# A gated S4 layer on one core: its hand-ordered list worked out anew, with the time steps' chain moved from VectorE to GpSimd

## The chip, the cores and the metric

The kernel runs on one core of one Trainium2 chip. The metric is the device time of one execution in microseconds; the figure given for a kernel is the median of its runs. The core's engines are named as in the profile: PE is the matrix engine (PEld its weight loads), DVE the vector engine, ACT the scalar engine, POOL the GpSimd engine, SP the engine that issues most DMAs. Each runs its own instructions in program order and waits for the others by semaphores.

## What is computed

A sequence of 2048 rows of 512 features is normalized row by row. One branch is a convolution along the sequence whose kernel is made from 512 x 128 complex parameters; the other is a feed-forward layer with 1792 hidden features. Their product is added to the input:

```python
xn = _layernorm(x, axis=-1)                       # x: (1, 2048, 512)
s  = _A_ref(xn, A_re, A_im, B_re, B_im, C_re, C_im, log_dt, Dskip)
#   dt = exp(log_dt); K[d,l] = Re sum_n C * dt*B * exp(dt*A*l); causal convolution of xn with K, + xn*Dskip
g  = _silu(_gelu(xn @ w1 + b1) @ w2 + b2)         # w1: 512 x 1792, w2: 1792 x 512
return x + s * g
```

## The kernel before

Three strands of work are woven into one list.

**Feed-forward.** x is cut into 4 tiles of 512 rows, the hidden features into 14 tiles of 128 (tiles 0 to 6 in a first pass over x, 7 to 13 in a second). Every float32 operand is split into a high and a low part, so that each product is three products of 128x128 with 512 columns ("wide products" below). Names in the code: `split` (L238, L240) casts a weight tile's high part on ACT and subtracts the low part on DVE, or on POOL where the list says so; `first_half` (L255 to L257) is 6 of the 12 products of a hidden tile, `first_start` (L265) the 12 of the very first; `gate` (L269) is gelu on ACT, `gate_high` (L275) the cast of its high part `hh`, `ffn_rest` (L281) the low part `hl` on DVE; `second_part` (L293 to L296) is 3 products into one of four sums `z`. Staging buffers for raw weights are four, so a load waits until an earlier tile has been split.

**Layer norm of x.** `ln_load` (L321) loads 128 x 2 rows, `ln_stat` (L326) takes statistics, `ln_root` and `ln_scale` normalize, `ln_store` (L356) stores the rows for the convolution, `ln_turn` (L368) transposes on PE, `ln_high` and `ln_low` (L377, L383) split. `ln_keep` (L387, L388) stores a whole split tile, 2 MB, from POOL's queue, for the second pass.

**The convolution's kernel.** `timestep` computes exp(log_dt) by a polynomial. `params` (token `P`) prepares the parameters of a block of 128 features on POOL, ACT and DVE, with six loads each. The generator then makes 32 sub-blocks: `gen_load` (`KL`), `gen_phase` (`A`, L599, PE), `gen_round` (`B`, L607 on ACT or L609 on DVE), `gen_wrap` (`C`, L613), `gen_size` (`Z`, L619 to L624, POOL), `gen_sin` (`N`, ACT), `gen_tables` (`E`, L645 to L652, DVE), `gen_sum` (`Q`, L660, PE), `gen_out` (`U`), `gen_keep` (`UD`).

The order of all this is the string `ORDER`: each token calls one of these functions, and the instructions of each engine follow each other as the tokens do. Nothing reorders them later. Before the list stands `prologue`, written out by hand: loads, dummy products on PE (`warm`), the time steps, the first x tile and the first hidden tile. The tokens met below: `F.j.h` first half h of step j; `G.j`, `H.j`, `R.j` gelu, high part, low part; `S.j.i` second half; `W.f`, `WB.f` the loads of w1 and w2 of hidden tile f; `WS.f.k` their four splits, a fourth number 1 meaning POOL; `LK.t` the store of a split x tile, `LL`, `LS`, `LD` load, statistics and store of rows; `B.s.h.o` rounds on DVE when o equals h and on ACT otherwise. After the list, from about 400 us on, the Fourier transforms of the convolution follow in a fixed order (`kernel_load` at L851 brings the finished kernel back, `side_skip` at L857 adds the skip, `first_dft` at L867 transforms).

Of the kernel before, what the change touches and what calls it, by code (L numbers as in the profile page):

```python
# [20 lines left out]
P = 128  # L21
# [30 lines left out]
WS.4.2 S.1.0 F.4.0 G.3 W.5 KL.0.0 H.2 H.3 LR.2 KL.0.1 S.1.1 KL.1.0 P.0 P.0 F.4.1 R.2 G.4 P.1 WS.3.3 LC.2  # L52
WS.4.3 S.1.2 S.1.3 S.2.0 Z.0 WB.5 S.2.1 TF.2.0 LC.3 A.0.0 TH.2.0 W.6 S.2.2 TF.3.0 R.3 LS.5.0 KL.1.1
B.0.0.1 H.4 WS.5.0 TL.2.0 C.0.0 S.2.3 S.3.0 WB.6 TH.3.0 WS.6.0 LS.4.0 TF.2.1 R.4 A.0.1 P.1 TL.3.0 S.3.1
S.3.2 B.0.1 WS.6.1 S.3.3 TH.2.1.1 WS.5.1 WS.5.2.1 TF.3.1 TL.2.1 S.4.0 C.0.1 WS.6.2 TH.3.1 TL.3.1 F.5.0
LS.5.1 N.0.0 A.1.0 F.5.1 B.1.0 F.6.0 C.1.0 A.1.1 N.0.1 LS.4.1 S.4.1 LR.4 B.1.1 LD.3 C.1.1 KL.2.0 G.5
E.0.0 E.0.1 N.1.0 E.0.2 F.6.1 S.4.2 G.6 LD.2 H.5 KL.3.0 R.5 S.4.3 H.6 A.2.0 F.7.0 B.2.0.1 F.7.1 LC.5
C.2.0 WS.5.3 F.8.0 N.1.1 Q.0 F.8.1 S.5.0 A.2.1 LC.4 S.5.1 G.7 WS.6.3.1 B.2.1 R.6 H.7 G.8 P.0 KL.2.1 Z.1
E.1.0 S.5.2 E.1.1 S.5.3 TF.4.0 C.2.1 S.6.0 E.1.2 TH.4.0 A.3.0 N.2.0 B.3.0.1 S.6.1 TL.4.0 F.9.0 Z.2 R.7
H.8 F.9.1 KL.4.0 U.0 O.0.0 C.3.0 KL.3.1 P.1 TF.4.1 S.6.2 A.3.1 G.9 P.1 F.10.0 O.0.2 B.3.1.1 O.0.1 C.3.1  # L60
LD.4 Q.1 N.2.1 S.6.3 A.4.0 R.8 F.10.1 O.0.3 E.2.0 S.7.0 Z.3 S.7.1 UD.0 E.2.1 E.2.2 LD.5 S.7.2 N.3.0 S.7.3
TH.4.1 H.9 S.8.0 U.1 UD.1 KL.5.0 B.4.0 LL.6 Q.2 N.3.1 S.8.1 G.10 R.9 C.4.0 TL.4.1 S.8.2 A.4.1 F.11.0
E.3.0 B.4.1 E.3.1 U.2 H.10 F.11.1 S.8.3 C.4.1 N.4.0 E.3.2 KL.4.1 R.10 P.1 TF.5.0 G.11 A.5.0 Q.3 TF.5.1
TH.5.0 S.9.0 S.9.1 B.5.0 KL.6.0 C.5.0 TL.5.0 LK.1 TH.5.1 F.12.0 TL.5.1 P.1 A.5.1 N.4.1 H.11 S.9.2 B.5.1
P.1 F.12.1 S.9.3 LL.7 C.5.1 F.13.0 P.1 KL.5.1 Z.4 G.12 N.5.0 H.12 R.11 P.1 S.10.0 P.1 S.10.1 LS.6.0
LS.6.1 N.5.1 F.13.1 S.10.2 G.13 F.14.0 KL.7.0 KL.6.1 P.1 LK.2 F.14.1 Z.5 R.12 S.10.3 A.6.0 U.3 F.15.0
S.11.0 E.4.0 E.4.1 G.14 E.4.2 B.6.0 C.6.0 LS.7.0 S.11.1 S.11.2 UD.3 UD.2 A.6.1 LS.7.1 Q.4 P.1 S.11.3
B.6.1 E.5.0 F.15.1 KL.7.1 Z.6 H.13 S.12.0 C.6.1 R.13 LR.6 E.5.1 A.7.0 H.14 F.16.0 E.5.2 S.12.1 B.7.0 OK.0
U.4 N.6.0 N.6.1 R.14 S.12.2 S.12.3 C.7.0 F.16.1 LC.6 P.2 E.6.0 G.15 P.2 E.6.1 S.13.0 P.1 S.13.1 Z.7 G.16
O.1.0 KL.8.0 A.7.1 F.17.0 LD.6 S.13.2 B.7.1 H.15 R.15 S.13.3 TF.6.0 F.17.1 H.16 C.7.1 O.1.1 KL.8.1 O.1.2  # L70
TH.6.0 G.17 A.8.0 TL.6.0 Q.5 P.2 O.1.3 E.6.2 TF.6.1 P.2 B.8.0 N.7.0 UD.4 R.16 U.5 TH.6.1 N.7.1 F.18.0
S.14.0 C.8.0 S.14.1 F.18.1 E.7.0 S.14.2 G.18 Q.6 A.8.1 S.14.3 S.15.0 LC.7 TL.6.1 B.8.1.1 Z.8 C.8.1 U.6
KL.9.0 W.7 P.2 S.15.1 WB.7 S.15.2 KL.9.1 H.17 TF.7.0 S.15.3 E.7.1 P.2 F.19.0 A.9.0 S.16.0 W.8 F.19.1 R.17
# [98 lines left out]
def kernel(  # L172
# [508 lines left out]
    def prologue():  # L681
# [17 lines left out]
        for n in range(2, 4):  # L699
            ln_load(n)  # L700
# [477 lines left out]
```

## Time and profile before

| | |
|---|---|
| time, median of 3 runs | 572.32 us (569.98 to 574.2) |
| the profiled execution | 573.57 us, of which the span from first to last instruction is 571.8 us |
| mean granted clock of PE | 0.99 |
| instructions | 17148 |

A page of the profile gives busy time by engine, the span in 40 slices, DMA queues, and groups of instructions by line. Views of the trace give the same for a stretch of time, the instructions in order, and for each idle stretch of an engine what ended it ("<-"). In the view by stretches the columns are the engines' busy times, the clock granted to PE (1.00 is full speed), the share of time that the DMA engines were busy, and GB/s. An engine with a small q behind its name is its sequencer, issuing a DMA.

### The profile page before, as it was taken

Reading aid. Unit: us, or ns where it says so; the run is one execution under the profiler, and the core shown is the slowest. Engines: PE = TensorE matmul, PEld = TensorE weight load, DVE = VectorE, ACT = ScalarE, POOL = GpSimd, SP = SyncE. Lnnn points to the kernel's source line nnn. Section 1 sums busy time; section 2 is a strip of 40 time slices with the busy share of each in tenths; the row PEclk is TensorE's granted clock in tenths of the full one; section 3 lists DMA queues with packets and bytes.
Section 4 is the critical chain, followed back from the end, with each engine's and each line's share of the span. In section 5 each row is a group of like instructions: output and inputs, shape, how many; then the busy total and the mean of one; then the engine's idle time right before and its main releaser. Section 6 shows DMA issues by size and latency. Waiting matters only on the chain. (4 is left out here: it accounts for less than half of the span.)

```text
span 571.8 us, 17148 instructions
## 1 busy us (share of the span) xinstructions
PE 545.7 (95%) x7187; PEld 436.7 (76%) x7187; DVE 468.6 (82%) x721; ACT 410.8 (72%) x599; POOL 282.5 (49%) x379
## 2 busy tenths in 40 slices
PE   8759999998999999999999999999999999999995
PEld 8548777766777777777777777777889988987883
DVE  6859999999998999999988988985357656766875
ACT  3538987987877999798998789698255556564542
POOL 0617483654874578969917746740320304114423
PEclk9889999999999999999999999999999999999999
DMA  8994235653376343474088106703976483625945
GB/s 189 263 294 133 74 92 206 211 192 89 114 279 223 130 139 97 162 204 74 4 270 293 47 21 147 147 10 101 381 288 77 129 134 77 188 51 120 206 114 110
DMA packets 99129, 86.92 MB, mean 152 GB/s; under 512 B 44294, under 2 KB 87562, under 8 KB 95980
## 3 DMA queue, kind: packets, MB, share of 16 engines
q1 hardware_dynamic: 94512, 65.37, 43.1%
q0 software_dynamic: 3424, 19.93, 10.1%
q8 instruction: 56, 0.92, 0.7%
q10 hardware_dynamic: 1116, 0.53, 0.4%
q14 instruction: 21, 0.17, 0.1%
HBM read 52.25 MB, written 33.55 MB: 150 GB/s over the span
## 5 line engine op out<-in xcount | busy, mean ns | idle before, releaser
L622 POOL TENSOR_TENSOR mm<-mm,rc 128x32 f32<-128x32 f32 (+4 forms) x150 | 112.9, 752 | 11.8
L255 PE MATMUL f<-xh,w1h 128*128 128x512 f32 x220 | 93.5, 425 | 5.8 <-ACT hf L269 5.8
L294 PE MATMUL z<-w2h,hh 128*128 128x512 f32 x224 | 97.8, 436 | 0.0
L257 PE MATMUL f<-xh,w1l 128*128 128x512 f32 x220 | 87.9, 399 | 2.5 <-DVE w1l L240 2.5
L295 PE MATMUL z<-w2l,hh 128*128 128x512 f32 x224 | 88.9, 397 | 0.0
L296 PE MATMUL z<-w2h,hl 128*128 128x512 f32 x224 | 88.5, 395 | 0.0
L256 PE MATMUL f<-xl,w1h 128*128 128x512 f32 x220 | 87.5, 398 | 0.0
L886 PE MATMUL s<-X,mc 64*64 64x128 f32 x2048 | 64.3, 272 | 1.1 <-issue 0.9
L903 DVE TENSOR_TENSOR t<-s,uh 128x512 f32<-128x512 f32 x64 | 41.1, 684 | 27.9 <-ACT uh L894 27.5
L886 PEld LDWEIGHTS s<-X,mc 64*64 64x64 f32 x2048 | 56.4, 133 | 5.4 <-issue 3.2
L281 DVE TENSOR_TENSOR hl<-hf,hh 128x512 fp32r<-128x512 f32 x56 | 50.5, 903 | 9.5 <-ACT hh L275 9.5
L619 POOL COPY mm<-rc 128x32 f32<-128x32 f32 x30 | 11.1, 370 | 91.5 <-DVE e L652 51.8
L255 PEld LDWEIGHTS f<-xh,w1h 128*128 128x128 f32 x220 | 42.0, 191 | 15.5 <-ACT hf L269 6.4
L257 PEld LDWEIGHTS f<-xh,w1l 128*128 128x128 f32 x220 | 41.8, 190 | 13.0 <-DVE w1l L240 2.9
L296 PEld LDWEIGHTS z<-w2h,hl 128*128 128x128 f32 x224 | 42.2, 189 | 10.4 <-DVE hl L281 0.4
L294 PEld LDWEIGHTS z<-w2h,hh 128*128 128x128 f32 x224 | 42.7, 191 | 9.3
L295 PEld LDWEIGHTS z<-w2l,hh 128*128 128x128 f32 x224 | 42.6, 190 | 8.2
L256 PEld LDWEIGHTS f<-xl,w1h 128*128 128x128 f32 x220 | 41.8, 190 | 8.9
L645 DVE TENSOR_TENSOR e<-mm,ra 128x1024 f32<-128x1024 f32 x32 | 44.4, 1388 | 4.2 <-ACT ra L633 3.9
L873 ACT COPY X<-s 128x512 f32<-128x512 f32 x56 | 28.9, 599 | 25.1 <-PE s L867 25.1
L613 DVE SCALAR_TENSOR_TENSOR ra<-ra,ph 128x512 f32<-128x512 f32 x64 | 43.6, 681 | 3.6 <-ACT ra L607 2.6
L269 ACT ACTIVATE hf<-f,b1s 128x512 f32<-128x512 f32 x56 | 38.5, 690 | 10.4 <-PE f L257 4.6
(181 smaller groups left out, 1161.9 us busy)
## 6 DMA issues: line engine op xcount, KB each, us to landing
x<-in_A_u_dram SPq DMA_DIRECT2D x16, 256.0 KB
xs<-x SPq DMA_DIRECT2D x16, 256.0 KB
xt_h<-xh POOLq DMA_DIRECT2D x4, 1024.0 KB, 6.1
xt_l<-xl POOLq DMA_DIRECT2D x4, 1024.0 KB, 8.1
kgd<-ko SPq DMA_DIRECT2D x32, 128.0 KB
za<-zo SPq DMA_DIRECT2D x4, 1024.0 KB
xh<-xt_h POOLq DMA_DIRECT2D x4, 1024.0 KB, 5.2
xl<-xt_l POOLq DMA_DIRECT2D x4, 1024.0 KB, 7.9
```

What stands on the lines that cost most here:

```text
L255: PE.matmul(p, wh[:, k, :], xh[:, k, :], start=(k == 0), stop=False)
L256: PE.matmul(p, wh[:, k, :], xl[:, k, :], start=False, stop=False)
L257: PE.matmul(p, wl[:, k, :], xh[:, k, :], start=False, stop=(k == KD - 1))
L281: V.tensor_sub(hl, hf, hh)
L294: PE.matmul(z, hh[:, s], wh, start=(f0 == 0 and not rows), stop=False)
L295: PE.matmul(z, hh[:, s], wl, start=False, stop=False)
L296: PE.matmul(z, hl[:, s], wh, start=False, stop=(f0 == FA - 1))
L613: V.scalar_tensor_tensor(ra[:, 0, c], ra[:, 1, c], MAGIC, p, op0=ALU.subtract, op1=ALU.subtract)
L622: GP.tensor_mul(mv[:, :, 0:3:2, w:2 * w], mv[:, :, 0:3:2, 0:w], rc[:, 2 + 2 * i:4 + 2 * i, :].rearrange("p j c -> p c j").unsqueeze(3).to_ ...
L645: V.tensor_mul(e1, m1.unsqueeze(1).to_broadcast([P, 2, CH, N1]), ra[:, :, :, :N1])
L886: PE.matmul(p[ka * 64:(ka + 1) * 64, r, o, :, jj], mc[h, k, ((0, 2), (1, 0))[c][o], :], xf[b][h, c, :, k, :], start=(c == 0), stop=(c == 1 ...
L903: V.tensor_mul(t, p[:, i, :, 1].unsqueeze(1).to_broadcast([P, 2, 2, P]), uh)
```

## The change

The list is written anew with the same tokens in another order, with a few marks changed. The hand-written part moves the time steps' arithmetic to POOL, runs 25 dummy products in place of 29, puts the load of the table `cbs` behind the parameters' and the next x rows, and takes the low row of b2 between the statistics.

```diff
 ORDER = """
-WS.0.3 LD.0 LD.1 WS.1.0 WS.1.1 P.0 P.0 W.2 G.0 H.0 WB.2 P.0 WS.1.2 W.3 BB P.0 R.0 P.0 WS.2.0 LS.3.0 F.1.0
-LL.4 LS.3.1 S.0.0 S.0.1 LS.2.0 WS.2.1 WS.1.3 WS.3.0 LS.2.1 WB.3 WS.2.2 S.0.2 F.1.1 LL.5 P.0 W.4 WS.2.3
-F.2.0 G.1 WS.3.1 H.1 WS.3.2 F.2.1 F.3.0 P.0 F.3.1 P.0 WB.4 S.0.3 P.1 WS.4.0 R.1 G.2 WS.4.1 P.0 LK.0 P.0
...
-S.52.2 S.52.3 G.55 R.54 S.53.0 UD.30 U.31 S.53.1 S.53.2 S.53.3 H.55 UD.31 R.55 KL0
+WS.0.3 LD.0 LD.1 P.0 WS.1.0 WS.1.1 P.0 P.0 WS.1.2.1 G.0 F.1.0 LS.2.0 W.2 LS.3.0 WB.2 H.0 W.3 P.0 WS.2.0
+LK.0 R.0 LL.4 LS.3.1 WS.1.3 P.0 WS.2.1 F.1.1 LS.2.1 G.1 WS.2.2 WS.2.3 P.0 S.0.0 WB.3 WS.3.0 W.4 WS.3.1
+S.0.1 H.1 F.2.0 S.0.2 F.2.1 G.2 WS.3.2 P.0 WB.4 H.2 W.5 WS.4.0 LL.5 F.3.0 P.0 WS.5.0 S.0.3 P.0 F.3.1 R.1
...
+N.31.1 E.31.0 U.29 E.31.1 G.54 F.55.1 Q.30 G.55 U.30 H.54 S.52.3 S.53.0 UD.29 E.31.2 Q.31 H.55 R.54 U.31
+S.53.1 S.53.2 S.53.3 UD.31 R.55 UD.30 KL0
 """
 def timestep():
...
-        V.tensor_scalar(x, p, -87.0, 88.5, op0=ALU.max, op1=ALU.min)
...
-        for c in (1.0 / 720, 1.0 / 120, 1.0 / 24, 1.0 / 6, 0.5, 1.0):
-            V.scalar_tensor_tensor(e, e, c, r, op0=ALU.add, op1=ALU.mult)
-            yield
...
+        A.copy(x, p)
+        yield
+        k, r, t, e = small("k"), small("r"), small("t"), small("e")
+        GP.tensor_scalar(x, x, -87.0, 88.5, op0=ALU.max, op1=ALU.min)
...
+        for c in (1.0 / 120, 1.0 / 24, 1.0 / 6, 0.5, 1.0, 1.0):
+            GP.tensor_mul(e, e, r)
+            GP.tensor_scalar(e, e, c, 1.0, op0=ALU.add, op1=ALU.mult)
...
 def prologue():
...
-        warm(29)
+        warm(25)
...
-        SY.dma_start(cbs, cb)
         next(pgen[0])
         for n in range(2, 4):
             ln_load(n)
+        SY.dma_start(cbs, cb)
         mv, rs = pair(0)
         bias_high()
-        for n in range(2):
-            ln_stats(n, mv[:, 2 * n:2 * n + 2, :])
+        ln_stats(0, mv[:, 0:2, :])
+        bias_low()
+        ln_stats(1, mv[:, 2:4, :])
...
-        bias_low()
         first_start(*steps[0])
```

In the whole list, 12 weight subtractions are marked for POOL, before 6; of the 64 roundings DVE has 38, before 41; the high parts of x on DVE are 3, before 2; two transposes of x take their bank from the generator's (`T`, before `TF`). The store LK.0 moves from behind F.3.1 to behind F.1.0 in the list, LK.1 from behind the fourth kernel sum (Q.3) to ahead of the first; the last weight load W.13 stands about 4 us of PE work before its cast, before about 12.6. b2's spread over the partitions (`BB`) and the second block's parameter loads move back.

More of the change, by code (lines that the diff above doesn't have):

```diff
@@ L54 @@
[L54 to L73, printed above, removed]
@@ new lines @@
+H.9 S.7.3 TH.4.1.1 KL.5.0 TF.5.0 KL.4.1 U.1 Q.2 TL.4.1 N.3.1 Z.3 A.4.0 TH.5.0 R.9 F.11.1 B.4.0.1 G.11
+E.3.0 LL.6 S.8.0 KL.5.1 TL.5.0 C.4.0 S.8.1 U.2 S.8.2 A.4.1 B.4.1 F.12.0 P.1 TF.5.1 TH.5.1 E.3.1 C.4.1
+S.8.3 E.3.2 S.9.0 A.5.0 P.1 N.4.0 UD.1 H.10 UD.2 B.5.0.1 C.5.0 H.11 KL.6.0 S.9.1 F.12.1 S.9.2 D Z.4 R.10
+A.5.1 S.9.3 G.12 P.1 H.12 TL.5.1 KL.6.1 LL.7 OK.0 S.10.0 Q.3 B.5.1 N.4.1 KL.7.0 S.10.1 P.1 R.11 S.10.2
+P.1 F.13.0 U.3 C.5.1 S.10.3 S.11.0 P.1 LK.2 LS.7.0 N.5.0 LS.6.0 N.5.1 E.4.0 S.11.1 P.1 E.4.1 S.11.2
@@ new lines @@
+A.8.1 UD.6 R.16 S.14.2 TF.6.1 KL.9.1 TL.6.0 F.18.0 OK.1 S.14.3 P.2 UD.5 P.2 B.8.1 C.8.1 N.7.1 F.18.1
+TH.6.1.1 S.15.0 A.9.0 TL.6.1 S.15.1 TF.7.0 E.7.0 H.17 S.15.2 E.7.1 E.7.2 P.2 G.18 B.9.0 C.9.0 S.15.3
+N.8.0 F.19.0 F.19.1 S.16.0 A.9.1 Z.8 TH.7.0.1 LD.7 N.8.1 Q.7 R.17 H.18 S.16.1 TL.7.0 S.16.2 KL.10.0
+B.9.1.1 C.9.1 G.19 LD.6 E.8.0 E.8.1 N.9.0 TF.7.1 S.16.3 U.7 F.20.0 H.19 W.7 A.10.0 KL.11.0 TH.7.1 KL.10.1
+S.17.0 F.20.1 E.8.2 Q.8 N.9.1 S.17.1 B.10.0 U.8 S.17.2 R.18 C.10.0 Z.9 S.17.3 G.20 TL.7.1 S.18.0 A.10.1
@@ new lines @@
+N.14.0 UD.10 E.13.1 W.11 UD.11 WS.8.2.1 U.12 E.13.2 S.25.1 N.14.1 KL.16.0 A.15.0 R.26 S.25.2 P.3 G.27
+F.28.1 KL.14.1 WS.9.1 XL.1 B.15.0 C.15.0 A.15.1 S.25.3 S.26.0 Z.14 F.29.0 WS.9.2 WS.10.1 S.26.1 WB.11
+S.26.2 B.15.1.1 KL.15.1 H.27 C.15.1 N.15.0 WS.8.3 G.28 H.28 UD.12 P.2 W.12 Z.15 F.29.1 Q.13 WS.11.0
+N.15.1 A.16.0 E.14.0 E.14.1 E.14.2 WB.12 F.30.0 R.27 KL.17.0 B.16.0.1 WS.11.1 S.26.3 WS.12.0 U.13 S.27.0
+C.16.0 KL.16.1 G.29 R.28 S.27.1 A.16.1 B.16.1 H.29 S.27.2 UD.13 WS.10.2.1 O.3.0 P.3 KL.18.0 F.30.1
@@ new lines @@
+E.19.1 A.21.0 S.34.2 H.36 ZA.0.2 R.36 G.37 F.38.0 F.38.1 N.20.0 S.34.3 Q.18 ZA.0.3 S.35.0 N.20.1 ZG.0
+KL.21.1 E.19.2 B.21.0 S.35.1 C.21.0 SL1.0 F.39.0 UD.16 S.35.2 E.20.0 S.35.3 U.18 G.38 XL.2 A.21.1 E.20.1
+E.20.2 Q.19 B.21.1 F.39.1 S.36.0 C.21.1 KL.22.0 U.19 S.36.1 A.22.0 H.37 R.37 H.38 N.21.0 Z.21 UD.19
+S.36.2 KL.23.0 R.38 G.39 B.22.0.1 C.22.0 Q.20 N.21.1 F.40.0 P.3 P.3 UD.18 A.22.1 S.36.3 F.40.1 H.39
+B.22.1 ZL.1 S.37.0 C.22.1 S.37.1 P.3 P.3 KL.22.1 P.3 F.41.0 U.20 G.40 E.21.0 F.41.1 S.37.2 KL.23.1 P.3
```

132 lines of the change are left out of this document (63 added, 69 removed).

## The prediction

> **What bounds the kernel now.** I read the busy shares first, then the same shares by stage with the granted clock, then the list of waits inside the worst stage, then the order in time around each wait.
>
> ```profile
> PE 545.7 (95%) x7187; PEld 436.7 (76%) x7187; DVE 468.6 (82%) x721; ACT 410.8 (72%) x599; POOL 282.5 (49%) x379
> ```
> ```profile
> 21.00:24.50 3.50, 2.88 (x7) 2.31 (x8) 3.43 (x7) 1.32 (x3) 2.89 (x7) 0.51 0.76 232
> 34.97:41.23 6.26, 0.51 (x3) 0.19 (x2) 0.61 (x1) 1.26 (x3) 0.22 (x1) 0.75 0.94 340
> 41.23:44.90 3.67, 3.67 (x9) 2.90 (x10) 3.39 (x13) 3.64 (x7) 2.83 (x7) 0.50 0.48 113
> 44.90:80.00 35.10, 35.10 (x224) 27.61 (x223) 34.47 (x60) 31.04 (x52) 22.36 (x29) 1.00 0.36 104
> 80.00:140.00 60.00, 54.93 (x538) 41.65 (x536) 57.19 (x92) 48.71 (x72) 34.04 (x53) 1.00 0.52 167
> 140.00:400.00 260.00, 259.64 (x2652) 199.22 (x2650) 234.13 (x308) 224.75 (x289) 167.44 (x214) 1.00 0.47 137
> 400.00:571.80 171.80, 161.85 (x3619) 139.77 (x3617) 110.61 (x166) 86.34 (x156) 44.22 (x50) 1.00 0.62 156
> ```
> Columns: stretch and length, then busy time of PE, weight load, DVE, ACT and POOL, granted clock, DMA share, GB/s. From 140 to 400 us PE has no gap (259.64 of 260): that stage costs what its products cost, and the new list has the same products. After 400 us the code is the same. So the list can win or lose in the first 140 us, or by starving PE where it is full now. Between 80 and 140 us PE is idle for 5.07 us while DVE is at 95%. The rest of the loss is in the first 45 us:
>
> ```profile
> ACT w1h L238 <- DMA w1s<-in_B_w_dram: 10.6, 3, 6.3
> PE f L255 <- ACT hf L269: 5.8, 1, 5.8
> PE f L257 <- DVE w1l L240: 2.5, 1, 2.5
> 27.09 0.54 SPq L221 DMA_DIRECT2D w1s<-in_B_w_dram  x1
> 28.00 0.76 POOL L387 DMA_DIRECT2D xt_h<-xh  x1
> DMA to landing us min/median/max: 11.5/11.5/11.5
> 39.97 0.62 ACT L238 CAST w1h<-w1s 128x512 fp32r<-128x512 f32 x1 [6.26 <-DMA w1s<-in_B_w_dram]
> ```
> PE's 5.8 us end with ACT's gelu (L269), but the gelu stood behind the cast of weight tile 4, which waited for its load: issued at 27.09, usable at 39.97, 12.9 us. One microsecond after it POOL issued the store of the first x tile (LK.0, L387 and L388); the landing row is the store of its low part, issued at 28.76, so it ended at 40.2. The load came in with the store, not before. The clock column adds a second cost: 0.51 after the wait at 21.6, 0.50 after the one at 41.2.
>
> ```profile
> 26.49 0.39 PE L255 MATMUL f<-xh,w1h 128*128 128x512 f32 x1
> 33.48 0.40 PE L294 MATMUL z<-w2h,hh 128*128 128x512 f32 x1
> 41.82 0.63 PE L256 MATMUL f<-xl,w1h 128*128 128x512 f32 x1
> 44.38 0.63 PE L295 MATMUL z<-w2l,hh 128*128 128x512 f32 x1
> 45.10 0.39 PE L255 MATMUL f<-xh,w1h 128*128 128x512 f32 x1
> ```
> The first two rows are 30 wide products apart: 0.233 us each. The next two are 6 apart: 0.427 us each at half clock. Before 45.10, 74 wide products have been issued. My sum compares the time of that 74th.
>
> **The change part by part.** *Start.*
>
> ```profile
> 4.56 8.07 PE L430 MATMUL warm<-ident 128*128 128x128 f32 x58
> 4.67 0.16 DVE L466 TENSOR_SCALAR sm_x<-sm_turn 128x4 f32<-128x4 f32 x1 [3.03 <-PE sm_turn L464]
> 7.01 0.69 DVE L326 BATCH_NORM_STATS2 bst<-x 128x6 f32<-128x512 f32 x1
> 12.80 2.03 PE L368 MATMUL xT<-ident,x 128*128 128x128 f32 x16 [0.17 <-DVE x L351]
> 15.60 1.20 PE L265 MATMUL f<-xh,w1h 128*128 128x512 f32 x4 [0.78 <-ACT xh L377]
> 0.00:5.00 5.00, 3.49 (x15) 3.25 (x16) 1.04 (x7) 1.67 (x3) 0.84 (x7) 1.00 0.56 136
> ```
> DVE's chain of 13 small operations for the time steps runs from 4.67 to 7.09, and the statistics of x start right behind it without waiting for data. By 5 us the DMAs have moved 136 GB/s x 5 = 680 KB, so the first x tile (512 KB, first in SP's queue) is in; the second follows by about 7. Without the chain, DVE has 2.3 us more, of which the row correction of b2 (0.68, moved between the statistics) takes part, and the second x tile the rest. The 25 warm products (50 of the 58 passes, 8.07 x 50/58 = 6.96) end at 11.5 instead of 12.6. I put the transposes at 11.55, 1.25 earlier (bounds 0.5 and 1.3, the warm products' end), and the first tile's product at 14.35.
>
> The chain itself is now 22 POOL operations. No such shape ran there:
>
> ```profile
> L857 POOL TENSOR_TENSOR in<-in,dsk x8: 227/228/232, 406.6 to 490.9; 128x16 f32<-128x16 f32 x8
> L530 POOL TENSOR_SCALAR pr_h<-pr_h 128x128 f32<-128x128 f32 x8 | 4.3, 533 | 0.7
> 14.19 0.46 POOL L500 TENSOR_TENSOR pr_wr<-pr_cr,pr_br 128x128 f32<-128x128 f32 x1 [12.74 <-DMA pr_br<-in_A_B_re_dram]
> 28.09 0.35 DVE L535 SCALAR_TENSOR_TENSOR pr_ci<-pr_ci,sm_dt,pr_br 128x128 f32<-128x128 f32 x1 [1.27 <-POOL pr_br L532]
> ```
> Between 22 x 0.228 = 5.0 and 22 x 0.533 = 11.7 us from 4.9 on; I take 0.25 each (nearest in size), so it ends near 10.5, inside POOL's wait until 14.19 (about 13.3 now that the table cbs is loaded behind the parameters). The result is first used at 28.09. At nothing, then; at the upper bound it delays POOL by 3 us. Its extra ACT copy lies in ACT's wait for b2.
>
> *First tile.*
> ```profile
> 20.87 0.69 DVE L240 TENSOR_TENSOR w1l<-w1s,w1h 128x512 fp32r<-128x512 f32 x1
> L240 POOL TENSOR_TENSOR w1l<-w1s,w1h x1: 1279/1279/1279, 52.2 to 52.2; 128x512 fp32r<-128x512 f32 x1
> 18.97 0.93 SPq L221 DMA_DIRECT2D w1s<-in_B_w_dram  x1
> 23.88 0.62 ACT L238 CAST w1h<-w1s 128x512 fp32r<-128x512 f32 x1 [2.17 <-DMA w1s<-in_B_w_dram]
> ```
> Weight tile 1's low part (L240, waited for 2.5 us by PE) goes from DVE at 20.87 to POOL, behind six parameter operations (6 x 0.533 = 3.2 us from 13.3): 16.5 + 1.3 = 17.8, just as PE asks for it. That wait goes. PE then runs both tiles' 24 products and three of the second half, 27 x 0.233 = 6.3, to 20.65. Next late is hl of tile 0, which now stands on DVE behind two statistics of x: about 21.5 by an estimate (DVE's six parameter operations from 16.9 on, 2.3 us, two statistics of 0.69 with their 0.18, and hl's 0.7), a wait of 0.85. Four more products end at 22.4. Then PE wants weight tile 2, which before came at 23.88 and now has LK.0 in its way: the store is moved up past tile 2's and 3's loads, to POOL's turn at about 18.0, a moment before SP issues the load at 18.97 (SP's pace there is set by the four stores of xs, which don't move).
>
> What that costs is not shown; bounds: at best it lands as now (23.9); at worst with the end of LK.0, as weight tile 4 did: 18.75 + 11.5 = 30.2. I take 27.5, since the store's bytes are few beside the load's in the first microseconds: in the old place its 2 MB took until 40.2 with all queues full. Cast and start: 28.2, a new wait of 5.8 us for PE. It brings the half clock with it: about 8 products at 0.427, 1.6 us more. The other 43 products to the 74th take 10.0. The loads of tiles 3 and 4 (tile 4 now ahead of b2b and of x 5, which is 0.75 MB less) come in behind the same store while PE works, and I let them cost nothing beyond; uncovered, each microsecond counts fully. 74th: 28.2 + 1.6 + 10.0 = 39.8, against 45.1: **5.3 us gained**; 2.6 with tile 2 at 30.2; 9 with it at 23.9, where tile 4 holds it.
>
> The Trainium skill, page "DMA: Bandwidth & Descriptors", section "Queues, rings and completion order", says that each DMA engine takes turns between the queue rows packet by packet. By that the load on SP's row would share with POOL's store and land well before its end, and the sum would be near the 9; the 12.9 us of weight tile 4 speak against it.
>
> *The rest of the list.* DVE gives up the chain, 6 of 21 weight subtractions (POOL then has 12) and 3 of 41 roundings (to ACT), and takes one cast of x from ACT:
>
> ```profile
> L609 DVE TENSOR_SCALAR ra<-ph 128x512 f32<-128x512 f32 x41 | 28.1, 686 | 8.2 <-PE ph L599 6.6
> L240 DVE TENSOR_TENSOR w1l<-w1s,w1h 128x512 fp32r<-128x512 f32 x9 | 7.0, 774 | 5.7 <-ACT w1h L238 5.7
> L240 POOL TENSOR_TENSOR w2l<-w2s,w2h 128x512 fp32r<-128x512 f32 x3 | 4.8, 1593 | 1.2 <-ACT w2h L238 1.2
> ```
> 6 x 0.77 + 2 x 0.69 = 6.0 us less on DVE beside the chain, some 3 of it due before 140 us. DVE set PE's 5.07 us of idle there, so I book 1.5 of those (from -3, if POOL's 6 x 1.6 = 9.6 us delay the size tables or LK.1, the second x tile's store, moved up from behind the fourth kernel sum to ahead of the first, delays the generator's loads, to +4).
>
> The Trainium skill, page "SBUF — State Buffer", section "Who interferes with whom", says a POOL operation that reads SBUF and a DVE operation with two SBUF inputs block each other for a whole instruction. By that the six moved subtractions would hold DVE for up to 6 x 1.3 = 7.8 us and undo their 4.6, which leads to the given-back rival below. The trace agrees as far as POOL's 1.593 us in the mean against 1.279 for the single one; it does not show who blocked whom.
>
> *End of the list.*
> ```profile
> 397.24 1.10 PE L660 MATMUL kg<-e,e 128*32 128x64 f32 x64
> 407.92 0.23 POOL L857 TENSOR_TENSOR in<-in,dsk 128x16 f32<-128x16 f32 x1 [1.13 <-DMA in<-kgd]
> 411.14 2.01 PE L867 MATMUL s<-fc,in 32*128 32x64 f32 x64
> ```
> After the last kernel sum (397.24) there were seven second-half blocks, now three: the first transform that needs the reloaded kernel comes 4 x 0.7 = 2.8 us sooner after that sum. Its input was ready 3.0 us ahead (408.15 against 411.14). The slack is used up; I book 0.5 (0 to 3).
>
> Sum: 5.3 + 1.5 - 0.5 = 6.3 us. The profiled execution took 573.57 us (span 571.8, 1.8 around it), so 567.3 on its scale; it lies 1.25 above the median of 572.32, so **566.0**.
>
> **The rivals.**
> *The load shares with the store* (tile 2 at 23.9): 9 + 1.5 - 0.5 = 10 us, 562. For it: tile 2's load, issued at 18.97, took 4.9 us in a full queue. Against: tile 4's 12.9.
> *The loads land with the store's end*: gain 2.6 + 0 - 0.5, 570. For it, the same 12.9; against, that the store starts among bytes of xs still to be moved.
> *The front's gain is given back*: DVE, 98% busy from 44.9 to 80 and 95% to 140, does not follow, and PE waits there for what it gained: 572. Against: DVE itself idled at 34.97 to 41.23 (0.61 busy).
> *Slower: a second-half load is caught.* The last weight tile (W.13) is now cast about 4 us of PE work after its issue, before 12.6 (counted in the list, 0.7 us a block). If a 1 MB transfer is under way, it takes 12.9 as tile 4 did: ACT stands 9 us with gelus behind it, PE waits as at 34.97, plus half clock (9 x 0.19 = 1.7): 573.57 - 6.3 + 10.7 = 578, 577 on the median's scale. It decides once that load takes more than some 10 us. Against: tile 12 had 3.9 us of cover before, and ACT waited for no weight load after 45 us (13.5 us in all, 10.6 of them between 15 and 45 and 2.9 at 8.99).
>
> **How the numbers follow.** Chances: forecast 0.45, sharing 0.17, store's end 0.14, given back 0.10, slower 0.14. A measurement here can tell about 1% (5.7 us) from no change. The forecast's own range is 562 to 570; the range 558 to 576 takes in the bounds 562 less the +4 of the middle, and most of the slower case. Faster by over 1%: two thirds of 0.45, and 0.17: 0.48. Slower by over 1%: 0.14 and a remainder of the given-back case, 0.16. Within 1%: 0.36.
>
> **What would show it.** Right: transposes at 11.5 to 12; no wait of PE on L240's low part of tile 1; a wait of some 3 to 8 us for tile 2 at 22, with a clock near 0.5 behind it; none of 5 us at tile 4; the 74th wide product near 40; PE full from 140. Wrong: a wait on a weight cast after 45 us, PE idle over 8 us between 80 and 140, or DVE under 90% there with PE waiting.

## The result and the profile after

The changed kernel takes 578.63 us (median of 4 runs, 578.27 to 583.11), the kernel before 572.08 in the same comparison: a ratio of 1.014, with a 95% interval of 1.010 to 1.018. The prediction was 566.0 in a range of 558 to 576. The change costs 6.5 us where 6.3 were to be gained.

The profiled execution took 583.11 us (span 581.3), the longest of the four; the others lie 4 to 5 us below it. The view by stretches, with the columns as before (busy time of PE, PEld, DVE, ACT, POOL; granted clock, DMA share, GB/s), shows where it went:

```profile
24.50:35.60 11.10, 4.25 (x10) 3.34 (x11) 3.41 (x11) 3.85 (x6) 2.02 (x6) 0.54 0.91 255
45.00:80.00 35.00, 34.05 (x259) 25.79 (x261) 34.17 (x57) 30.53 (x51) 22.75 (x34) 1.00 0.64 192
80.00:140.00 60.00, 59.46 (x590) 45.91 (x578) 56.41 (x97) 51.22 (x78) 44.16 (x59) 1.00 0.37 118
140.00:250.00 110.00, 109.94 (x1014) 84.80 (x1018) 104.39 (x131) 97.08 (x133) 85.52 (x103) 1.00 0.54 177
250.00:262.00 12.00, 9.97 (x155) 7.87 (x152) 11.10 (x15) 7.27 (x9) 8.46 (x10) 0.86 0.54 86
281.00:305.00 24.00, 15.76 (x178) 11.77 (x178) 12.37 (x25) 12.90 (x17) 7.50 (x12) 0.79 0.70 209
305.00:400.00 95.00, 95.00 (x881) 72.99 (x880) 78.61 (x102) 82.32 (x100) 53.79 (x72) 1.00 0.40 104
```

Three of these stretches have a clock under 1.00: the front, 250 to 262, and 281 to 305. In the last PE is busy for 15.76 of 24 us, and a mean clock of 0.79 means that (1 - 0.79) x 24 / 0.5 = 10 us of it ran at half speed. Before, PE was busy for all 24 there. Between 80 and 140, on the other hand, PE is now busy for 59.46 of 60 us (54.93 before).

How far each kernel is at a given piece of work shows gains and losses better than busy shares do. The table gives the start of the n-th wide product in us, from the two traces in order of time. The lists put other work between the products in another order, so differences of 1 to 2 us inside the list mean little; the 1344th stands eight before the list's last in both (the count takes in the eight products that add b2).

| wide product | 1 | 24 | 40 | 74 | 100 | 400 | 800 | 850 | 950 | 1344 | span |
|---|---|---|---|---|---|---|---|---|---|---|---|
| before | 15.6 | 25.1 | 28.8 | 44.8 | 52.0 | 142.6 | 255.1 | 268.9 | 295.6 | 413.1 | 571.8 |
| after | 15.5 | 20.9 | 34.9 | 44.4 | 53.0 | 140.1 | 249.5 | 268.2 | 306.6 | 422.5 | 581.3 |
| after - before | -0.1 | -4.2 | +6.1 | -0.4 | +1.0 | -2.5 | -5.6 | -0.7 | +11.0 | +9.4 | +9.5 |

The front gains 4.2, loses 10.3 and wins 6.5 back; the middle gains 6.6; and between products 800 and 950 the kernel loses 16.6 us, all of it after 250 us, where the kernel before had no gap. From the 1344th product on the two are alike (158.8 and 158.7 us).

The list of waits, PE's three largest (in all, how often, the longest), and SP's longest in the window from 262 to 300 us:

```profile
PE ph L596 <- DMA lh<-pcd: 8.2, 1, 8.2
PE f L256 <- ACT w1h L239: 7.6, 1, 7.6
PE ph L596 <- DMA rc<-recd: 2.0, 1, 2.0
```
```profile
SPq L447 <- ACT ko L663: 17.1, 1, 17.1
```

The first is `lh`, the 24 KB that `gen_load` brings for sub-block 22. It is small, and PE waits 8.2 us for it. The timeline of SP, which issues it, tells why (start, duration of the issue; after first, then before):

```profile
265.87 0.33 SPq L667 DMA_DIRECT2D kgd<-ko  x1
283.13 5.41 SPq L447 DMA_DIRECT2D gd<-zi  x4
288.64 2.30 SPq L588 DMA_DIRECT2D rc<-recd  x1
290.98 1.46 SPq L819 DMA_DIRECT2D raw<-xs  x1
292.49 2.81 SPq L667 DMA_DIRECT2D kgd<-ko  x1
295.40 0.68 SPq L582 DMA_DIRECT2D lh<-pcd  x1
```
```profile
268.20 0.68 SPq L585 DMA_DIRECT2D lh<-pcd  x1
...
286.39 4.79 SPq L446 DMA_DIRECT2D gd<-zi  x4
291.27 1.90 SPq L585 DMA_DIRECT2D lh<-pcd  x1
```

L447 is `z_store`, the second half of token `ZG.0`: four stores of 256 KB of what a silu on ACT has just made. SP comes to them at 266.2, stands 17 us until the silu is done, and issues nothing meanwhile. (The list of waits names ACT's copy to `ko`; the silu, L441 below, ended at 283.11, and the first store went out at 283.13.) Behind them in the new list stand `KL.21.1` (`rc`, the seeds of a size table), `SL1.0` (`raw`), `UD.16` (`kgd<-ko`, the store of a finished kernel block) and `KL.22.0` (`lh`). In the old list `KL.22.0` stood ahead of `ZG.0` and went out at 268.20. On ACT and PE the same thing is seen from the other side:

```profile
281.19 1.92 ACT L441 ACTIVATE zi<-zi 128x2048 f32<-128x2048 f32 x1
285.46 0.69 ACT L604 ACTIVATE ra<-ph,mag 128x512 f32<-128x512 f32 x1
297.08 0.37 ACT L663 COPY ko<-kg 128x256 f32<-128x256 f32 x1 [10.93 <-DMA kgd<-ko]
297.68 0.61 PE L596 MATMUL ph<-cbs,lh 96*128 96x512 bf16 x1 [8.24 <-DMA lh<-pcd]
```

ACT too stands 10.9 us, at `U.18`: its output buffer `ko` (two of them) is free only when `UD.16`'s store is through. And one more load is in play: `XL.2`, the reload of an x tile (2 MB on POOL's queue), starts at 282.3, ahead of these loads, where in the kernel before `lh` had gone out 17 us ahead of it (268.20 and 285.10). So two theories stood at this point. *SP's order*: one store that waits for an engine holds every load behind it in SP's queue. *The bytes*: 2 MB of reload and 1 MB of stores under way at once are what delays them. The front's loss (LK.0, as the prediction feared) was the second thing to test.

### The profile page after: what moved, and what is told of

Same layout as the page of the kernel before. It is cut to its first block, busy times and chain, and to the rows that moved or that the text cites. A ratio compares the mean times of both kernels' runs of the same rounds, so it can differ in the third digit from the quotient of the medians.

```text
span 581.3 us, 17142 instructions
## 1 busy us (share of the span) xinstructions
PE 545.8 (94%) x7179; PEld 435.7 (75%) x7179; DVE 461.2 (79%) x700; ACT 411.6 (71%) x601; POOL 296.9 (51%) x407
## 3 DMA queue, kind: packets, MB, share of 16 engines
q1 hardware_dynamic: 94512, 65.37, 42.7%
q0 software_dynamic: 3424, 19.93, 10.2%
## 4 chain that ended last, share of the span: by engine, by line
PE 57%; DVE 20%; ACT 6%; DMA 5%; issue 5%; SPq 4%; POOL 1%; DVEq 0%; POOLq 0%; ACTq 0%
PE s L883 7%; PE z L295 7%; PE z L296 6%; PE z L297 6%; PE f L256 5%; PE f L257 5%; PE f L258 5%; PE kg L657 4%; PE s L864 4%; PE sa L918 3%; DMA w2s<-in_B_w_dram 2%; DVE hl L282 2%; PE ph L596 2%; PE w L936 2%; DVE ra L610 1%
## 5 line engine op out<-in xcount | busy, mean ns | idle before, releaser
L619 POOL TENSOR_TENSOR mm<-mm,rc 128x32 f32<-128x32 f32 (+4 forms) x150 | 114.3, 762 | 11.8
L295 PE MATMUL z<-w2h,hh 128*128 128x512 f32 x224 | 99.0, 442 | 0.0
L282 DVE TENSOR_TENSOR hl<-hf,hh 128x512 fp32r<-128x512 f32 x56 | 49.1, 882 | 13.1 <-ACT hh L276 13.0
L616 POOL COPY mm<-rc 128x32 f32<-128x32 f32 x30 | 10.9, 364 | 80.5 <-DVE e L649 53.7
L295 PEld LDWEIGHTS z<-w2h,hh 128*128 128x128 f32 x224 | 42.9, 191 | 11.1 <-issue 2.3
L297 PEld LDWEIGHTS z<-w2h,hl 128*128 128x128 f32 x224 | 42.5, 190 | 11.5 <-DVE hl L282 1.0
L296 PEld LDWEIGHTS z<-w2l,hh 128*128 128x128 f32 x224 | 42.7, 191 | 8.2
L642 DVE TENSOR_TENSOR e<-mm,ra 128x1024 f32<-128x1024 f32 x32 | 46.1, 1439 | 1.0 <-ACT ra L630 0.5
```

Source lines behind the costliest of these rows:

```text
L282: V.tensor_sub(hl, hf, hh)
L295: PE.matmul(z, hh[:, s], wh, start=(f0 == 0 and not rows), stop=False)
L296: PE.matmul(z, hh[:, s], wl, start=False, stop=False)
L297: PE.matmul(z, hl[:, s], wh, start=False, stop=(f0 == FA - 1))
L619: GP.tensor_mul(mv[:, :, 0:3:2, w:2 * w], mv[:, :, 0:3:2, 0:w], rc[:, 2 + 2 * i:4 + 2 * i, :].rearrange("p j c -> p c j").unsqueeze(3).to_ ...
L642: V.tensor_mul(e1, m1.unsqueeze(1).to_broadcast([P, 2, CH, N1]), ra[:, :, :, :N1])
```

## The experiments

All kernels are compared with the kernel before on the same chip; its median was 571.0 to 572.2 us in the three groups of runs.

**Three tokens ahead of the silu's stores (a_keys).**
```diff
-... N.20.1 ZG.0 KL.21.1 E.19.2 ... F.39.0 UD.16 ... C.21.1 KL.22.0 U.19 ...
+... N.20.1 KL.21.1 UD.16 KL.22.0 ZG.0 E.19.2 ... F.39.0 ... C.21.1 U.19 ...
```


> The changed kernel with three tokens moved: KL.21.1 (load of the size table's seeds), UD.16 (store of a finished kernel block) and KL.22.0 (the load lh of sub-block 22) stand ahead of ZG.0 instead of behind it. Theory, SP's order: in the changed kernel SP stands from 266.2 to 283.1 at the four stores of ZG.0, which wait for the silu, and then issues seed load, raw load, block store and lh one behind the other until 295.4; PE, which wants lh at 289, stands 8.4 us and then runs 10 us at half clock. With the three ahead of the silu both go: product 950 comes no later than product 850 against the kernel before (now it loses 11.7 us between them), and the time is 578.6 - 11.7 = 567. Rival, the bytes: the reload of an x tile (XL.2, 2 MB) and the silu's 1 MB under way from 282 on are what holds the loads; then the wait moves to the next load or to ko's store and at least half of the loss stays: 573 or more.

Measured: 569.27 us (10 runs), ratio 0.997 (0.994 to 1.000). Product 850 stands at -1.4 against the kernel before, product 950 at +0.1. Between the two the kernel loses 1.5 us where the changed kernel loses 11.7, and SP's timeline has the three ahead of the stores:
```profile
265.64 0.38 SPq L588 DMA_DIRECT2D rc<-recd  x1
266.08 0.45 SPq L667 DMA_DIRECT2D kgd<-ko  x1
271.23 0.66 SPq L582 DMA_DIRECT2D lh<-pcd  x1
282.48 5.28 SPq L447 DMA_DIRECT2D gd<-zi  x4
```
SP still stands 11 us before the silu, and PE waits for nothing there. (The profiled execution of this kernel, 579.6 us, is the longest of its ten. Of its excess 6.6 us lie behind the list, with 10.2 us at half clock from 427 on, which the median does not show.)

**The reload later (a_xl).**
```diff
-... U.18 G.38 XL.2 A.21.1 ... S.36.1 A.22.0 H.37 ...
+... U.18 G.38 A.21.1 ... S.36.1 A.22.0 XL.2 H.37 ...
```


> The changed kernel with one token moved: the reload XL.2 (2 MB on POOL's queue) stands behind A.22.0 and no longer ahead of it, as in the kernel before; SP's order is that of the changed kernel. Theory, SP's order: SP still issues nothing between 266 and 283 and lh stands behind ZG.0's stores; only the issues after 288.6 (2.30, 1.46 and 2.81 us where such an issue takes 0.3 to 0.6 elsewhere) become quicker, by at most 5 us. PE still stands 3 to 5 us at sub-block 22, and the time is 574 to 577. Rival, the bytes: without the reload the loads come in time, PE doesn't stand there, and the time is 567.

Measured: 580.73 us, ratio 1.014 (1.009 to 1.018), the changed kernel's. PE waits as long as ever:
```profile
PE ph L596 <- DMA lh<-pcd: 8.5, 1, 8.5
```
The expectation, 574 to 577, missed as well: POOL has nothing to do between the two places, so the reload's two issues went out at 281.08 and 281.69, no later against the rest than in the changed kernel (282.34 and 282.95), and the slow issues behind the stores stayed. This run shows that the token's place doesn't matter, not what the kernel would do without those bytes. The bytes as the cause by themselves fall by the run above: there the reload is where the changed kernel has it, and the loss is gone. A share in it they may have: behind the stores the three issues ahead of `lh` took 6.6 us together in the changed kernel, where such an issue mostly takes 0.3 to 0.6, so by an estimate some 5 of the 8.2 us are slow issues. They matter only for what stands behind the stores, and no run takes the bytes away.

**The reverse, in the kernel before (b_zg).**
```diff
-... A.21.1 KL.22.0 ZA.0.3 ... P.3 ZG.0 H.38 A.22.0 ...
+... A.21.1 ZA.0.3 ... P.3 ZG.0 KL.22.0 H.38 A.22.0 ...
```


> The kernel before with one token moved: KL.22.0 (lh of sub-block 22) stands behind ZG.0, whose four stores wait for the silu, and no longer ahead of it. Nothing else of the change is in it. Theory, SP's order: lh is issued at about 291.2, behind the stores (they end there in the kernel before), and lands 2.2 us later; A.22.0 wants it at 285.7, so PE stands 7 to 9 us and then runs 3.4 to 10 us at half clock, 2 to 5 us more: 571.6 + 10 to 13 = 582 to 585. Rival, that the late wait of the changed kernel needs its other moves too (the reload XL.2, UD.16's store): then PE stands less than 3 us and the time is 575 or less.

Measured: 583.65 us, ratio 1.021 (1.015 to 1.026): one token makes the kernel before 11.5 us slower, without anything else of the change. The token now stands two ahead of its use, so this run alone does not tell the stores from the short distance; a_actq below does.
```profile
PE ph L599 <- DMA lh<-pcd: 10.9, 2, 10.6
```
Product 900 stands at -3.4 and product 950 at +9.3: 12.7 us lost at this place.

**The load of sub-block 22 alone (a_kl22).**
```diff
-... N.20.1 ZG.0 KL.21.1 ... C.21.1 KL.22.0 U.19 ...
+... N.20.1 KL.22.0 ZG.0 KL.21.1 ... C.21.1 U.19 ...
```


> The changed kernel with KL.22.0 alone ahead of ZG.0; the block store UD.16 and the seed load KL.21.1 stay behind it. Theory: PE's wait of 8.4 us for lh goes, but ACT still stands at ko (U.18) until UD.16's store has landed near 297, with the casts of hh behind it, and POOL at the seeds until 295.7; PE runs out of second halves some 5 us later and stands 3 to 6 us for hl. About half of the 11.7 us comes back: 572 to 574, and PE's wait there is on DVE's hl or ACT's hh. Rival, lh alone made the loss: no wait over 2 us between 280 and 305, and the time is that of the kernel with all three moved, 569.

Measured: 579.17 us, ratio 1.012 (1.007 to 1.016). Nothing came back that the measurement could tell, where I had expected half; neither forecast time was met. The wait moved:
```profile
ACT ko L663 <- DMA kgd<-ko: 10.9, 1, 10.9
DVE hl L282 <- ACT hh L276: 10.4, 1, 10.4
PE kg L657 <- ACT ko L663: 7.1, 1, 7.1
```
The next kernel sum (`kg`, one PSUM buffer) needs ACT's copy of the sum before it, the copy needs a `ko` buffer, and that buffer's store is `UD.16`, still behind the silu. The mechanism was right, its way to PE was another (the sum's buffer, not `hl`), and its size was 7.1 us rather than 3 to 6. Both things behind `ZG.0` cost PE about the same 7 to 8 us; to move one of them gains nothing.

**The stores on ACT's queue (a_actq).**
```diff
-            (GP if t == NTB - 1 else SY).dma_start(gd[b]...
+            (GP if t == NTB - 1 else A).dma_start(gd[b]...
```


> The changed kernel with its own list; the four stores of a ZG go out on ACT's queue, behind the silu that makes them, and not on SP's. Theory, SP's order: SP no longer stands at the silu, so seeds, raw rows, ko's store and lh go out as they come due, and PE's wait of 8.4 us at sub-block 22 goes without any token moved; ACT pays some 1 to 5 us for issuing the four, of which PE sees little. The time is 568 to 572. Rival, the bytes or the list's order itself: the wait stays above 4 us and the time is 575 or more.

Measured: 574.83 us, ratio 1.006 (1.002 to 1.009); against the changed kernel's 1.014, so by the medians rather more than half comes back with the list untouched, though the time is 3 us above the 572 expected at most. PE no longer waits for `lh`, whose token still stands three ahead of its use: SP issues it 20 us before PE comes to it (290.72). But ACT pays for issuing the stores, seen in its timeline and in PE's waits:
```profile
270.12 0.68 SPq L582 DMA_DIRECT2D lh<-pcd  x1
281.38 4.93 ACTq L447 DMA_DIRECT2D gd<-zi  x4
```
```profile
PE kg L657 <- ACT ko L663: 3.1, 1, 3.1
```
Four issues hold ACT 4.9 us, the upper end of the price that I had set (1 to 5 us); "of which PE sees little" was wrong, PE waits 3.1.

**The store of x at its old place (a_lk).**
```diff
-... WS.2.0 LK.0 R.0 LL.4 ... F.3.1 R.1 P.0 WS.4.1 ...
+... WS.2.0 R.0 LL.4 ... F.3.1 R.1 P.0 LK.0 WS.4.1 ...
```


> The changed kernel with one token moved: LK.0 (the 2 MB store of the first split x tile) stands behind R.1, as in the kernel before, and no longer ahead of the loads of weight tiles 2 and 3. Theory: weight tile 2 lands near 24 as in the kernel before and not at 30.6; PE's wait of 7.6 us and two of its three stretches at half clock go, product 74 comes at 35 to 38 (now 44.4), and most of it stays to the end: 569 to 573. Rival, given back: DVE, busy 34.17 of 35 us between 45 and 80, does not follow; product 74 comes early but product 400 at 139 or later, and the time is 577.

Measured: 575.99 us, ratio 1.007 (1.005 to 1.010), 2.6 us below the changed kernel. Product 74 comes at 36.2 as expected, PE's wait for tile 2 is 0.8 us; but product 100 comes at 47.8: of 8.2 us gained, 5.2 are left. Product 400, at 134.4, still has them, as the first theory said; the time, expected at 569 to 573, lies nearer to the rival's 577. Part of the difference is that the changed kernel's profiled execution is 4.5 us above its median, so that a gain read against it is too large.

**The store of x moved up, in the kernel before (b_lk).**
```diff
-... BB P.0 R.0 P.0 WS.2.0 ... WS.4.1 P.0 LK.0 P.0 ...
+... BB P.0 LK.0 R.0 P.0 WS.2.0 ... WS.4.1 P.0 P.0 ...
```


> The kernel before with one token moved: LK.0 stands ahead of R.0, POOL's sixth parameter operation behind it, so that POOL issues the 2 MB store at about 17.5, as in the changed kernel. Theory, the loads land with the store's end: weight tile 2 comes at 30 to 31 in place of 23.9, PE stands 6 to 8 us there and none at weight tile 4 (now 5.8); one wait for another, product 74 at 44 to 47 (now 44.8), the time 571 to 574. Rival, what the prediction took (tile 2 at 27.5, the wait at tile 4 gone): product 74 near 42, the time 569. Rival, sharing: tile 2 at 24, product 74 at 39, the time 566.

Measured: 571.85 us, ratio 1.000 (0.997 to 1.003). This is the move on which the prediction's largest term rests, by itself, and it is worth nothing.
```profile
29.62 0.62 ACT L238 CAST w1h<-w1s 128x512 fp32r<-128x512 f32 x1 [7.89 <-DMA w1s<-in_B_w_dram]
```
Tile 2 came at 29.62, 0.8 us behind the store's end (28.83), as the first theory had it, and ACT's wait at tile 4 shrank from 6.3 to 1.8. But PE stood only 1.9 us for tile 2, not 6 to 8, and product 74 came at 41.9, where the rival that stands for the prediction had it (near 42). The time is the first theory's. This profiled execution, 569.38, is the shortest of its ten.

**Both (a_all).** LK.0 as in a_lk, the three tokens as in a_keys, and `KL.20.0` ahead of `ZL.0 SL1.2`.


> The changed kernel with both: LK.0 behind R.1; KL.21.1, UD.16 and KL.22.0 ahead of ZG.0; and KL.20.0 (lh of sub-block 20) ahead of ZL.0 and SL1.2, behind whose 256 KB of small packets it now stands (PE stands 2.0 us for it at 254 and runs 3.4 us at half clock). Theory: the three losses are apart in time and add: 11.7 + 3 to 5 + 6 to 9, so 553 to 558. Rivals: if the front's gain is given back, 562; if bytes and not SP's order make the late losses, 569 or more.

Measured: 567.86 us (10 runs), ratio 0.992 (0.989 to 0.995): faster than both kernels, but 10 us short of the sum that I expected.
```profile
250.00:262.00 12.00, 12.00 (x112) 9.43 (x105) 10.62 (x16) 10.10 (x13) 5.63 (x10) 1.00 0.85 156
281.00:305.00 24.00, 23.36 (x220) 17.97 (x219) 20.19 (x39) 21.94 (x35) 11.31 (x16) 1.00 0.63 182
```
Both late gaps are closed, and the clock never falls before the last 3.4 us. By medians 578.6 - 569.3 = 9.4 for the three tokens and 2.6 for LK.0 make 12.0, and 10.8 is measured; for `KL.20.0`, which has no run of its own, nothing is left that could be told. What I had wrong were the sizes: I took them from the profiled execution of the changed kernel, which lies 4.5 us above its median, and the front gave back.

**LK.0 later still (a_lk2).** As a_all, with `LK.0` behind `Z.0`.


> The changed kernel with the three tokens ahead of ZG.0, KL.20.0 ahead of ZL.0, and LK.0 later still: behind Z.0, near 48 us, when the weights of tiles 2 to 6 have landed. Behind R.1 (the run with both) the store caught weight tile 5: ACT stood 5.7 us for it, DVE 2.1 us for x, and 4 of the 8 us gained by product 74 were gone at product 100. Theory: these go, product 100 comes at 44 to 46 (47.8 there), and the time is 564 to 566. Rival: the store now meets the second x tile's (LK.1 at 57) and holds the generator's loads; then product 150 is where it was (61) or later, and the time is 568 or more.

Measured: 567.57 us, ratio 0.992 (0.988 to 0.997), as a_all. ACT no longer waits 5.7 us for tile 5, and product 100 still comes at 48.0. The first theory falls: the store at its old place is not what sets that point. The rival's collision is not seen either (product 150 at 61.4, 61.1 in a_all).

**Two subtractions back to DVE (a_dve), two more to POOL (a_relief).**
```diff
 a_dve:    WS.4.3.1 -> WS.4.3     WS.3.3.1 -> WS.3.3      (from a_all)
 a_relief: WS.4.2 -> WS.4.2.1     WS.2.3 -> WS.2.3.1      (from a_all)
```


> The kernel with both (LK.0 behind R.1, the loads ahead of ZG.0, KL.20.0 earlier) with two of its marks taken away: the low parts of weight tiles 4 and 3 (WS.4.3, WS.3.3) are subtracted on DVE, not on POOL. Theory, DVE sets the front from about 40 us on (product 100 came at 47.8 to 48.0 in three kernels whose product 74 came between 36.2 and 38.6): product 100 comes 1 to 2 us later, near 49.3, and the time is 569 to 570. Rival: POOL's subtractions hold DVE for as long as they save it; product 100 within 0.5 us of 47.8, the time 568.

> The kernel with both, with two marks more: WS.2.3 and WS.4.2 (low parts of weight tiles 2 and 4) on POOL, which stands idle from 29 to 39 us there. Theory, DVE sets the front: two subtractions of 0.69 less, product 100 near 46.5, the time 566 to 567. Rival: POOL's subtractions hold DVE as long as they save it, or ACT, busy 3.97 of 4 us from 40 to 44, takes its place: product 100 within 0.5 us of 47.8, the time 568.

Measured: 568.15 us, ratio 0.994 (0.991 to 0.997), and 566.43, ratio 0.991 (0.988 to 0.994); product 100 at 47.9 and 48.7. The intervals of all four versions overlap, and product 100 doesn't follow the marks either way, so the first theory's path falls in both. The times leave more open: a_relief's 566.43 is what the first theory forecast, and it lies 1.7 us below a_dve, four subtractions away, little more than the scatter of the runs. Where such a gain would arise no trace shows. In a_all ACT is as full as DVE in this stretch, in a_lk2 DVE alone is full (columns as above; a_all, then a_lk2):
```profile
40.00:52.00 12.00, 9.28 (x47) 6.66 (x47) 11.27 (x20) 11.39 (x26) 10.55 (x15) 1.00 0.73 206
```
```profile
40.00:52.00 12.00, 12.00 (x54) 8.99 (x53) 11.89 (x18) 9.12 (x19) 10.55 (x16) 0.87 0.82 260
```
With ACT at 11.39 of 12 or DVE at 11.89, six kernels (these four, a_lk and b_zg) reach product 100 between 47.6 and 48.7. Which of the two would have to give way is left open.

**The hand-written start alone (b_start).** The old list behind the new start.


> The list of the kernel before behind the changed kernel's hand-written start (time steps on POOL, 25 dummy products, cbs's load later, b2's low row between the statistics). Theory: the first wide product comes at 15.4 to 15.6, as in the changed kernel (before 15.6), since the x rows land at 5.7 and not by 5, and ACT's four casts of x set the end of it; the start is worth less than 0.5 us and the time is 571 to 573. Rival, the prediction's 1.25 us: first wide product at 14.4, the time 570 to 571. Rival, POOL's chain in DVE's way: first wide product after 16, the time 573 or more.

Measured: 569.37 us (10 runs) against 570.96, ratio 0.999 (0.996 to 1.002). First wide product at 15.3. The start is worth nothing that can be told here.

## Why the prediction was wrong

It said rightly that the list "can win or lose in the first 140 us, or by starving PE where it is full now", and then looked for starving loads among the weights alone. Its slower rival was of the right kind and put at the wrong load; that its 577 lies near the measured 578.6 is luck. One small sum is off: two thirds of 0.45, and 0.17, make 0.47 and not 0.48. Point by point:

- **Start, -1.25: measured -0.1.** The step that failed here is the landing of x. Statistics began at 5.76 and not at 4.67, so scaled x came 0.3 us earlier, and ACT's four casts of it took 0.2 longer:
```profile
5.76 0.69 DVE L327 BATCH_NORM_STATS2 bst<-x 128x6 f32<-128x512 f32 x1 [4.13 <-DMA x<-in_A_u_dram]
12.46 2.33 PE L369 MATMUL xT<-ident,x 128*128 128x128 f32 x16 [1.93 <-DVE x L352]
13.15 2.26 ACT L378 CAST xh<-xT 128x512 fp32r<-128x512 f32 x4 [2.75 <-PE xT L369]
```
  To conclude from 680 KB moved by 5 us that the first 512 KB issued are in takes it that the bytes arrive in the order of issue. In the clean test b_start statistics began at 5.75 as well, and no gain can be told.
- **POOL's chain at nothing: right.** It ran from 4.92 to 11.62, 0.3 us an operation where 0.25 was taken, and POOL's next work waited for a load until 12.51.
- **Tile 1's low part: right.** POOL made it from 16.17 to 17.46, PE's 2.5 us are gone and product 24 comes 4.2 us earlier. The wait for `hl` of tile 0 was 0.56, predicted 0.85.
- **The wait for tile 2: right in kind, short in size.** Estimated to land at 27.5 with 30.2 as the worst; ACT's cast started at 30.68, 12.4 us after the issue and 2.3 us behind the store's end (28.38). In the four other kernels with this front it started at 29.2 to 30.9, 0.6 to 1.4 us behind the store's end. The wait was 7.6 us instead of 5.8 (5.7 to 7.4 in those four). The half clock behind it was the larger error: 1.6 us were booked, one stretch of 3.4 us, as after the first wait of before; it lasted 10.2 us ((1 - 0.54) x 11.1 / 0.5) and cost 5:
```profile
30.68 0.62 ACT L239 CAST w1h<-w1s 128x512 fp32r<-128x512 f32 x1 [9.09 <-DMA w1s<-in_B_w_dram]
31.35 0.79 PE L256 MATMUL f<-xh,w1h 128*128 128x512 f32 x1 [7.56 <-ACT w1h L239]
```
  The Trainium skill's rule of turns between queue rows ("DMA: Bandwidth & Descriptors", "Queues, rings and completion order"), by which tile 2 would have come well before the store's end, is not borne out by this load nor by b_lk's. The rule agrees better with b_zg's tile 4, used at 33.50, 5.6 us before its store's end.
- **The 74th product at 39.8: measured 44.4** (42.7 to 45.4 in the four others). And the 44.8 that it was held against is not a property of the kernel before. b_zg's program is the same up to 268 us, and there the 74th product came at 37.0: its load of tile 4 went out at 26.97 and was used at 33.50, where the profile of before has 27.09 and 39.97. The gain was reckoned against a wait of 5.8 us that an execution may or may not have (b_start, with the same list, has one of 5.0). In four kernels that gained 6 to 9 us by product 74 (a_lk, a_all, a_lk2, b_zg) about 4 were left at product 100; that is, for half of it, the prediction's given-back rival, to which it gave 0.10.
- **80 to 140 us, +1.5: too little.** PE's idle time there fell from 5.07 to 0.54 us, and from product 100 to 800 the new list gains 6.6. This gain is in every execution: the four with the old list take 202.6 to 204.2 us for these products, the ten with the new one 195.9 to 196.6. That DVE set the idle time was read rightly: in the kernel before PE's waits there are 3.8 us for DVE's `ra` and 1.2 for its `e`, after the change 0.3 for `ra`. Whether DVE's lighter load, the cause given, removed them is not shown: with two of the early marks taken back (a_dve) product 400 came no later (134.4 against 134.9 in a_all), and the rest of the marks and the order of the list were not tested apart.
- **End of the list, -0.5: measured 0.1.**
- **What is missing from the sum.** 4.9 us between products 800 and 850 and 11.7 between 850 and 950. The step that failed, and that turned the gain into a loss, is the sentence that puts the list's effect past 140 us at nothing but W.13's chance of being caught. The cover of a weight load was counted in PE's work between its token and its use, and W.13 was indeed not caught. For the small loads no such count was made, and by itself it would not have told: `KL.22.0` stood 28 tokens ahead of its use and now stands three, and a_actq leaves it at three and issues it 20 us early, since SP runs ahead of PE as far as its queue lets it. What counts is whether a DMA stands between that waits for an engine. The diff showed `ZG.0` passing `KL.22.0`, `UD.16` and `KL.21.1`; I had not followed SP's own order through the list. The 4.9 us are smaller and their cause is in part open. PE stood 2.0 us for `lh` of sub-block 20 (the list of waits names `rc`, but the product reads `lh`) and ran 3.4 us at half clock. SP had stood 4.6 us until PE's phase product before was done, issued `lh` at 251.33, and it was used 4.8 us later, with 256 KB of raw rows issued ahead of it. With `KL.20.0` ahead of the raw rows (a_all) the stretch has no gap; but neither has it in a_kl22, which leaves the token, and in a_lk2, a_dve and a_relief a gap of some 2 us remained there, waiting for DVE.

Shown, then: the loss between products 850 and 950 comes from SP's order (a_keys, b_zg, a_actq); LK.0's move is worth nothing in the old list and costs 2.6 us in the new one by medians (b_lk, a_lk); the start is worth nothing that can be told. By medians, 9.4 + 2.6 of loss against 6.5 measured leaves some 5 us that the rest of the new list gains.

## What to carry to other kernels

For each queue that issues DMAs in order, list what it waits for: a store that waits for a computation is a wall, and every load that moves from ahead of it to behind it is late by that whole wait, however small it is. When one such load is cleared, look for the next thing behind the wall before expecting a gain (here a buffer's store, through ACT and one PSUM bank, cost the same 7 us). And before a wait in one profile is booked as a gain, see whether a second execution has it.

## What the runs showed of the hardware

**The half clock lasts longer than the gap.** In the traces it comes in stretches of 3.4, 6.8 or 10.2 us. Of the 16 gaps of 2.0 to 2.5 us on PE in all traces, eight were followed by 3.4 and seven by nothing (a_dve at 248, a_all at 415), as was one of 3.1 us (a_actq at 284); the remaining one, by 10.2, is in the long execution of a_keys. Gaps of 5.0 to 10.6 us were followed by 6.8 or 10.2 us, though PE then worked without a gap: the row from 281 to 305 in the first view holds one. So 8 us of idle cost 11 to 13. The Trainium skill, "TensorE: Matmul & The Clock Gate", section "What's actually happening", gives windows of about 3.4 us, a fall after an idle window and full speed after one busy window; the multiples of 3.4 agree, the falls after 2.0 us and the second and third stretch at half clock do not.

**DVE's two-input operations are longer beside POOL's.** Of the changed kernel's 56 `hl` subtractions on DVE, the 13 with no POOL work beside them took 0.685 us in the mean, the 43 others 0.941, though 14 of these stayed under 0.72. One stretch of a_lk2 shows a long one: DVE's `hl` overlaps the last of five operations of POOL that take 4.94 us together (the next five take 3.30):
```profile
246.84 1.60 DVE L282 TENSOR_TENSOR hl<-hf,hh 128x512 fp32r<-128x512 f32 x1
242.94 4.94 POOL L619 TENSOR_TENSOR mm<-mm,rc 128x32 f32<-128x32 f32 x5
```
That agrees with the rule of the Trainium skill ("SBUF — State Buffer", "Who interferes with whom") that the prediction cited. It could explain why product 100 does not follow the marks in a_dve and a_relief, a subtraction given to POOL being paid back by DVE's others; no run shows that.

**A load and a store on two queues share unevenly, and not the same way each time.** The same load, issued one microsecond ahead of the same 2 MB store, took 12.9 us to use in one execution (before) and 6.5 in another (b_zg).
